# Loading a set of attention rows by one transfer, and paying with a stepped VectorE write

## The chip, the cores and the metric

The kernel runs on one core of one Trainium2 chip. The metric is device time in microseconds (us): the median of several executions of the whole program. Five engines work side by side, each taking its own instructions in a fixed order: TensorE (PE in the profile; its weight loads are PEld), VectorE (DVE), ScalarE (ACT), GpSimd (POOL) and SyncE (SP). They meet at semaphores. SP, ACT and POOL also issue transfers, which 16 shared DMA engines carry out.

## The reference

The program has two stages. The first is attention with hashed masking: `q`, `k`, `v` have 4 batches, 8 heads, 768 tokens, 64 features. Six projections of each `q` and `k` row give six sign bits, a query sees only the keys with the same six bits, and a softmax over these weights the values.

```
q_bits = (einsum('bhsd,dk->bhsk', q, proj) > 0)          # the same for k
mask   = q_bucket[:, :, :, None] == k_bucket[:, :, None, :]
scores = where(mask, (q @ k.T) / 8, -1e9)
attn   = softmax(scores);  x = attn @ v                   # heads side by side: 3072 x 512
h      = max(x @ w1, x @ w2, x @ w3)                      # 512 -> 768
out    = h @ w_out                                        # 768 -> 512
```

The second stage is a feed-forward block over the 3072 rows of `x`, with a maximum over three products in the place of an activation.

## The kernel before

**Sets.** The queries or the keys ("one side") of four heads make a set, and there are eight quads of heads, `g` = 0 to 7, two to a batch. Batch 0 (quads 0 and 1) is loaded and transposed in another way, by pairs of heads on TensorE. For quads 2 to 7 a set passes through these steps, and the change touches the first two:

- `load_quad` brings a set into a tile `nat` of 128 partitions, 32 for each head, with 24 tokens of 64 features in each partition. It does so with four transfers, one for each head (L194).
- `turn` (L200) is a VectorE stream transpose of 32x32 blocks, from `nat` to the tile T32, where features are on partitions and tokens run along the row. One turn writes 128x384 in fp32, so a set has four turns: two halves of the features by two halves of the tokens.
- `narrow` (L205) is a GpSimd pass that scales T32 to bf16, after every second turn.
- `place` (L210) sends the result by four transfers from SP into S, the operand of the score matmuls.
- `quad_hash` (L219) takes the turned tiles of both sides of a quad, computes their projections with eight matmuls on TensorE, has VectorE make bits of the signs (L222), and returns a function that sends the bits by four transfers from SP (L230) into eight extra rows of S. With those rows in the contraction, tokens of different buckets get scores that the exponential takes to almost nothing.

**Units.** The attention is cut into 192 units, 48 to a batch. A unit is one head with 768 columns of scores: two or three matmuls (L296) and one exponential on ScalarE (L304). Batch 0 has three chunks of 256 queries, the others two of 384. A loop over the units issues first the scores of the next unit, then whatever a table `at` holds for this unit, then pieces of the feed-forward block as a credit allows (L406 for the first layer, with VectorE's maxima at L415 and copies at L413; L450 for the second, with ScalarE's copies at L454), then sums (L351) and values (L373) of heads that are done, and last the hash, if `hash_at` names one for this unit. Sums of weights over tokens are prepared by VectorE (L327, L330), and VectorE also divides (L358 to L380).

The order of every engine is thus written out by hand: `when(u, ...)` puts a step at a unit, and the position in the loop is the position in each engine's queue. A load of quads 4 to 7 is issued by POOL, 14 to 11 units ahead of the set's first turn, one head to a unit; the loads of quads 2 and 3 come from SP, but for the queries of quad 2, which come from POOL. The turns of quads 4 to 7 are spread at two and a quarter or three units from each other (`SPREAD`). The hash of quad 3 stands at unit 48, behind the sums and values that end batch 0. Its bits are first needed by unit 60, whose scores are issued at unit 59.

**Buffers that matter.** Four PSUM banks (`bank`, `give`) serve all matmuls except the scores: TensorE can begin a group only when VectorE or ScalarE has emptied the bank that comes free next. The scores have two PSUM buffers of their own. `nat` has six buffers, T32 and its bf16 copy three each, S six.

Of the kernel before, what the change touches and what calls it, by code (L numbers as in the profile page):

```python
# [17 lines left out]
def kernel(  # L18
# [12 lines left out]
    nc = tc.nc  # L31
    B, H, S, D = q.shape
# [3 lines left out]
    HALF = S // 2  # L36
# [4 lines left out]
    Q = 32  # L41
    CC = P // Q
# [55 lines left out]
    nat, t32, t16, s_of, where, v_at = {}, {}, {}, {}, {}, {}  # L98

    def start_set(name, heads):  # L100
        nat[name] = nat_pool.tile([P, 4 * NM * D], FP32, tag="nat", name="nat")
        for x, key in enumerate(heads):
            where[key] = (name, x)
# [7 lines left out]
    def load_pair(pi, eng, sides=(1, 0), h0=0, h1=2):  # L111
        if pi not in nat:
            start_set(pi, [(0, 2 * pi), (0, 2 * pi + 1), (1, 2 * pi), (1, 2 * pi + 1)])
        n = nat[pi].rearrange("p (s h w) -> p s h w", s=2, h=2)
        for side in sides:
            src = (q, k)[side][0, 2 * pi + h0 : 2 * pi + h1].rearrange("h (p c) d -> p h (c d)", p=P)
            eng.dma_start(n[:, side, h0:h1, :], src)
# [66 lines left out]
        give(i)  # L184


    def load_quad(side, g, xs, eng):
        if (side, g) not in nat:
            start_set((side, g), [(side, 4 * g + x) for x in range(4)])
        for x in xs:  # L190
            b, h = divmod(4 * g + x, H)
            src = (q, k)[side][b, h].rearrange("(cc t m) d -> t cc (m d)", cc=CC, t=Q)
            dst = nat[side, g][x * Q : (x + 1) * Q, :].rearrange("t (cc w) -> t cc w", cc=CC)
            eng.dma_start(dst, src)  # L194

    def turn(name, u, half):
        if name not in t32:
            t32[name] = t32_pool.tile([P, 2, S], FP32, tag="T32", name="T32")
        i_ = nat[name].rearrange("p (cc m u d) -> p u m cc d", cc=CC, u=2, d=Q)[:, u, half * MH : (half + 1) * MH]
        nc.vector.transpose(t32[name][:, u, half * HALF : (half + 1) * HALF], i_)  # L200

    def narrow(name, u):
        if name not in t16:
# [268 lines left out]
    def when(u, f, *args):  # L472
        at.setdefault(u, []).append(lambda: f(*args))

    with tc.manual_schedule():
# [7 lines left out]
        load_pair(1, nc.sync)  # L483
        load_pair(2, nc.sync)
        load_pair(3, nc.sync)
        load_quad(1, 2, range(4), nc.sync)
        nc.vector.memset(pj2[:], 0.0)
        nc.vector.memset(ones[:], 1.0)
        for t in at_tiles:
# [67 lines left out]
        when(17, load_v, 1)  # L557
        for n, u in ((0, 3), (1, 12), (2, 21), (3, 31)):
            when(u, load_weights, n)
        when(13, load_quad, 0, 2, range(4), nc.gpsimd)  # L560
        for u, side, g in ((23, 1, 3), (27, 0, 3)):
            when(u, load_quad, side, g, range(4), nc.sync)
        hash_at = {}
        for g in range(2, NQUAD):
            b2, i2 = divmod(g, 2)
            need = UPB * b2 + 12 * i2
            for n, side in enumerate((1, 0)):
                name = (side, g)
                if g > 3:
                    us = [SPREAD[b2][0] + SPREAD[b2][1] * (8 * i2 + 4 * n + n2) // 4 for n2 in range(4)]  # L570
                    for x in range(4):
                        when(us[0] - 14 + x, load_quad, side, g, (x,), nc.gpsimd)
                else:
                    us = [need - {2: 26, 3: 23}[g] + 4 * n + n2 for n2 in range(4)]
                for n2, u2 in enumerate(us):
                    when(u2, turn, name, n2 // 2, n2 % 2)
                    if n2 % 2:
                        when(u2 + 1, narrow, name, n2 // 2)
                when(us[3] + 3, place, name, range(4))
            hash_at[{2: 32, 3: 48, 4: need - 12}.get(g, need - 9)] = g  # L580
            when({2: 36, 3: 46}.get(g, need - 22), load_v, g)

        ffn, credit = [], 0
# [2 lines left out]
        for c, i in sorted(done_at, key=lambda e: done_at[e]):  # L586
            d = done_at[c, i] + LAG[c > 2]
            sums, values = burst(c, i)
            pieces = [lambda f=sums: f(0, NM), lambda f=values: f(0, 0, NM), lambda f=values: f(1, 0, NM)]
            for n, f in enumerate(pieces):  # L590
                u = {(0, 0): (16, 17, 20), (1, 0): (21, 22, 24), (2, 0): (26, 27, 29)}.get((c, i), (d, d, d))[n]
# [67 lines left out]
```

## Time and profile before

| What | Value |
|---|---|
| median of 3 executions | 268.19 us (267.94 to 268.28) |
| the profiled execution, its own time | 268.58 us |
| span of its instructions | 266.6 us |
| busy PE / DVE / ACT / POOL | 257.9 / 208.9 / 177.3 / 69.9 us |
| the 48 turns (L200) on DVE | 27.0 us busy, 565 ns each |
| the 36 set loads issued by POOL (L194) | 20.0 us busy, 560 ns each |
| mean DMA rate over the span | 116 GB/s |
| granted TensorE clock | 1.0 |

Between the profiled execution's own time and its span lie 1.98 us, ahead of the first instruction and behind the last. The profiled execution is 0.39 us over the median. How to read the rest: a group line gives source line, engine, operation, shape and count, then total busy time and the mean time of one; waits name the engine that came last by the profile; the chain is what ended last, followed back in time from the last instruction. Busy times of a window table are sums within each stretch of the span.

### The profile page before, as it was taken

What the parts mean: (1) busy time and instruction counts of PE and PEld (TensorE: products, weight loads), DVE (VectorE), ACT (ScalarE), POOL (GpSimd) and SP (SyncE); (2) the same over time, 40 slices, a digit from 0 to 9 for tenths busy, and PEclk for the clock granted to TensorE, in tenths of its full rate; (3) what the DMA queues carried; (4) which work ended last, traced back from release to release, by engine and by line L of the source; (5) the groups of instructions that cost most, each with busy time, mean ns of one, the idle gap of its engine ahead of it and who ended that gap; (6) DMA issues with size and microseconds to landing.
All of it is one profiled execution on the core that took longest, in us unless ns stands there. A gap on an engine that the chain in (4) does not pass through costs nothing.

```text
span 266.6 us, 6482 instructions
## 1 busy us (share of the span) xinstructions
PE 257.9 (97%) x2505; PEld 154.4 (58%) x2505; DVE 208.9 (78%) x493; ACT 177.3 (67%) x257; POOL 69.9 (26%) x132
## 2 busy tenths in 40 slices
PE   7899999999799999999999999999999999999995
PEld 4555557885566575555555554555555555554552
DVE  2897685987499999978998997899849785888361
ACT  3596785676758694984869578484895859581322
POOL 3588652355032535240141612011000000000000
PEclk9999999999999999999999999999999999999999
DMA  6977999969703791982054472802030003000303
GB/s 203 316 156 135 230 234 212 245 114 233 185 22 86 159 231 18 234 222 53 4 167 131 56 182 43 204 8 61 15 118 4 0 2 119 2 0 2 118 0 118
DMA packets 20717, 30.95 MB, mean 116 GB/s; under 512 B 2608, under 2 KB 15248, under 8 KB 20688
## 3 DMA queue, kind: packets, MB, share of 16 engines
q0 software_dynamic: 8128, 13.37, 26.6%
q1 hardware_dynamic: 12128, 16.66, 21.8%
q10 hardware_dynamic: 432, 0.52, 0.6%
q8 instruction: 19, 0.31, 0.5%
q14 instruction: 10, 0.08, 0.1%
HBM read 25.17 MB, written 6.29 MB: 118 GB/s over the span
## 4 chain that ended last, share of the span: by engine, by line
PE 84%; DVE 7%; ACT 5%; issue 3%; DVEq 0%; ACTq 0%
PE ms L406 31%; PE sc L296 21%; PE ms L373 11%; PE ms L450 10%; ACT AT L304 4%; PE ms L351 3%; PE ms L219 3%; DVE ht L415 2%; DVE ad L327 1%; PE ms L498 1%; PE ms L122 1%; PE ms L149 1%; DVE T L131 1%; PE ms L169 1%; DVE S L174 1%
## 5 line engine op out<-in xcount | busy, mean ns | idle before, releaser
L304 ACT ACTIVATE AT<-sc 128x768 f16<-128x768 f32 x192 | 152.3, 816 | 62.2 <-PE sc L296 60.7
L406 PE MATMUL ms<-xT,w_sb 128*128 128x384 f16 (+1 forms) x648 | 114.8, 307 | 0.1
L296 PE MATMUL sc<-S 72*128 72x384 bf16 (+1 forms) x432 | 93.6, 308 | 3.3 <-ACT AT L304 1.8
L406 PEld LDWEIGHTS <-w_sb 128*128 128x128 f16 x648 | 62.7, 97 | 35.9 <-issue 0.4
L415 DVE TENSOR_TENSOR ht<-ht,ms 128x384 f16<-128x384 f16 (+1 forms) x108 | 54.3, 504 | 24.4 <-PE ms L406 13.4
L296 PEld LDWEIGHTS <-S 72*128 72x128 bf16 (+1 forms) x432 | 39.4, 98 | 35.7 <-issue 15.5
L205 POOL TENSOR_SCALAR T<-T 128x768 bf16<-128x768 f32 x24 | 22.8, 952 | 95.4 <-issue 50.5
L450 PE MATMUL ms<-wout_sb,ht 128*128 128x512 f16 x138 | 35.5, 378 | 0.0
L373 PE MATMUL ms<-AT,vo 128*32 128x385 f16 (+3 forms) x864 | 35.2, 309 | 0.3 <-DVE ht L415 0.3
L327 DVE TENSOR_TENSOR ad<-ad,AT 128x768 f16<-128x768 f16 x48 | 26.6, 553 | 2.1 <-ACT AT L304 1.3
L373 PEld LDWEIGHTS <-vo 128*32 128x32 f16 x864 | 22.6, 96 | 9.6 <-issue 1.8
L200 DVE STREAM_TRANSPOSE T<-nat 128x384 f32<-128x384 f32 x48 | 27.0, 565 | 0.2 <-DMA nat<-in_q_dram 0.2
L327 DVE TENSOR_TENSOR ad<-AT,AT 128x768 f16<-128x768 f16 x48 | 26.2, 546 | 0.2 <-ACT AT L304 0.2
L411 ACT CAST ht<-ms 128x384 f16<-128x384 f32 x36 | 17.3, 479 | 8.1 <-PE ms L406 8.1
L380 DVE SCALAR_TENSOR_TENSOR xT<-ms,sv,rb 128x384 f16<-128x384 f32 (+1 forms) x36 | 19.8, 567 | 1.4
L450 PEld LDWEIGHTS <-ht 128*128 128x128 f16 x138 | 13.3, 97 | 13.0 <-issue 0.3
L454 ACT COPY osb<-ms 128x512 f32<-128x512 f32 x21 | 12.2, 585 | 8.2 <-PE ms L450 6.3
L330 DVE TENSOR_TENSOR ad<-ad 128x384 f16<-128x384 f16 x32 | 15.5, 484 | 1.1
L136 POOL TENSOR_SCALAR S<-T 64x384 bf16<-64x384 f32 (+1 forms) x23 | 14.2, 617 | 5.0 <-DVE T L131 3.5
L358 DVE STREAM_TRANSPOSE ys<-ms 128x384 f32<-128x384 f32 (+1 forms) x18 | 9.6, 532 | 6.2 <-PE ms L351 6.2
L194 POOL DMA_DIRECT2D nat<-in_q_dram x20 | 11.1, 560 | 0.1
L413 DVE CAST ht<-ms 128x256 f16<-128x256 f32 x18 | 7.4, 413 | 4.0 <-PE ms L406 3.9
(48 smaller groups left out, 123.0 us busy)
## 6 DMA issues: line engine op xcount, KB each, us to landing
out_dram<-osb SPq DMA_DIRECT2D x21, 256.0 KB
S<-T SPq DMA_DIRECT2D x48, 96.0 KB
nat<-in_q_dram POOLq DMA_DIRECT2D x20, 192.0 KB, 6.7
vo<-in_v_dram POOLq DMA_DIRECT2D x8, 384.0 KB, 6.2
nat<-in_k_dram POOLq DMA_DIRECT2D x16, 192.0 KB, 5.7
w_sb<-in_moe_w_dram POOLq DMA_DIRECT2D x3, 768.0 KB, 6.9
nat<-in_k_dram SPq DMA_DIRECT2D x10, 192.0 KB
nat<-in_k_dram SPq DMA_DIRECT2D x3, 384.0 KB
```

The costliest lines, as they stand in the source:

```text
L200: nc.vector.transpose(t32[name][:, u, half * HALF : (half + 1) * HALF], i_)
L205: nc.gpsimd.tensor_scalar(out=t16[name][:, u, :], in0=t32[name][:, u, :], scalar1=RS, scalar2=1.0, op0=AluOp.mult, op1=AluOp.mult)
L296: nc.tensor.matmul(views[j], s_of[kn][0 : D + bits, kx, m * P : (m + 1) * P], s_of[qn][0 : D + bits, qx, q0 : q0 + w], start=True, stop=True)
L304: nc.scalar.activation(t[:, :, 0:w], whole, ActFn.Exp, bias=-SCALE * 0.25 * bits, scale=SCALE)
L327: nc.vector.tensor_tensor(out=sum_of[c, h][:], in0=t[0], in1=t[n], op=AluOp.add)
L330: nc.vector.tensor_tensor(out=t[:, 0, :], in0=t[:, 0, :], in1=t[:, 1, :], op=AluOp.add)
L373: nc.tensor.matmul(av[Q * x : Q * (x + 1), 0:n], v_at[2 * b + i][:, x, cb * D + side : (cb + 1) * D : 2], weights_of(c, 4 * i + x, m)[:, 0 ...
L380: nc.vector.scalar_tensor_tensor(out=xt_of(c)[:, 2 * i + side, 0:w], in0=av[:, 0:w], scalar=sv_of[b, i, side][:], in1=rb[0][:, 0:w], op0=A ...
L406: nc.tensor.matmul(ps[:, 0:w], w_sb[wi][:, jc, fb * P : (fb + 1) * P], xt[:, jc, 0:w], start=(jc == 0), stop=(jc == NJC - 1))
L411: nc.scalar.copy(hts[fb][:, 0:w], ps[:, 0:w])
L415: nc.vector.tensor_tensor(out=hts[fb][:, 0:w], in0=hts[fb][:, 0:w], in1=ps[:, 0:w], op=AluOp.max)
L450: nc.tensor.matmul(ps[:, 0:DM], hts[fb][:, tb * P : (tb + 1) * P], wout_sb[:, fb, :], start=(fb == 0), stop=(fb == NFB - 1))
```

## The change

A set is loaded by one transfer. A partition of `nat` now holds 24 tokens that follow one another in memory (6 KB in one piece), where before it held four groups of six tokens, 192 tokens apart (four pieces of 1.5 KB). The token that a partition and place hold is therefore another one; for S to keep its order, `turn` now writes its blocks interleaved: successive elements of a row go to addresses four fp32 words apart, in place of next to each other. Reads, shapes and everything behind T32 stay as they are.

The one transfer of quads 4 to 7 is issued 13 units ahead of the first turn, and the hash of quad 3 goes from unit 48 to unit 47, which puts its eight matmuls and its VectorE step ahead of the sums and values that end batch 0.

```diff
-    def load_quad(side, g, xs, eng):
-        if (side, g) not in nat:
-            start_set((side, g), [(side, 4 * g + x) for x in range(4)])
-        for x in xs:
-            b, h = divmod(4 * g + x, H)
-            src = (q, k)[side][b, h].rearrange("(cc t m) d -> t cc (m d)", cc=CC, t=Q)
-            dst = nat[side, g][x * Q : (x + 1) * Q, :].rearrange("t (cc w) -> t cc w", cc=CC)
-            eng.dma_start(dst, src)
+    def load_quad(side, g, eng):
+        start_set((side, g), [(side, 4 * g + x) for x in range(4)])
+        b, h = divmod(4 * g, H)
+        eng.dma_start(nat[side, g][:], (q, k)[side][b, h : h + 4].rearrange("h (t m) d -> (h t) (m d)", t=Q))
...
-        nc.vector.transpose(t32[name][:, u, half * HALF : (half + 1) * HALF], i_)
+        o = t32[name][:, u, half * HALF : (half + 1) * HALF].rearrange("p (m t cc) -> p m cc t", cc=CC, t=Q)
+        nc.vector.transpose(o, i_)
...
-        load_quad(1, 2, range(4), nc.sync)
+        load_quad(1, 2, nc.sync)
...
-        when(13, load_quad, 0, 2, range(4), nc.gpsimd)
+        when(13, load_quad, 0, 2, nc.gpsimd)
         for u, side, g in ((23, 1, 3), (27, 0, 3)):
-            when(u, load_quad, side, g, range(4), nc.sync)
+            when(u, load_quad, side, g, nc.sync)
...
-                    for x in range(4):
-                        when(us[0] - 14 + x, load_quad, side, g, (x,), nc.gpsimd)
+                    when(us[0] - 13, load_quad, side, g, nc.gpsimd)
...
-            hash_at[{2: 32, 3: 48, 4: need - 12}.get(g, need - 9)] = g
+            hash_at[{2: 32, 3: 47, 4: need - 12}.get(g, need - 9)] = g
```

On VectorE's queue the order of the steps is unchanged but for the one hash step (L222), which moves from behind the division of the last burst of batch 0 to ahead of it. POOL issues 9 set loads in place of 36, SP 3 in place of 12.

## The prediction

> **What bounds the kernel now.** I read the page's first parts, then who waits for whom, then the chain in order of time, then busy times by stretch.
>
> ```profile
> span 266.6 us, 6482 instructions
> ...
> PE 257.9 (97%) x2505; PEld 154.4 (58%) x2505; DVE 208.9 (78%) x493; ACT 177.3 (67%) x257; POOL 69.9 (26%) x132
> ...
> PE   7899999999799999999999999999999999999995
> PEld 4555557885566575555555554555555555554552
> DVE  2897685987499999978998997899849785888361
> ```
>
> PE is full but for the start, the end and one dent, slice 10 of the second part (about 67 to 73 us). A change can gain only there, or lose by holding PE up. The waits of PE between 60 and 80 us name the dent:
>
> ```profile
> PE sc L296 <- ACT AT L304: 1.5, 1, 1.5
> ```
>
> The chain shows the same place, and what comes behind it (start, duration, what):
>
> ```profile
> 70.13 0.82 ACT AT L304
> 70.95 1.00 issue
> 71.95 0.48 PE sc L296 x2
> 74.05 0.57 DVE T L200
> 76.44 0.49 DVE T L200
> 77.71 0.50 DVE ys L358
> ```
>
> ACT is named, but its last exponential ended at 70.95, and PE went on a whole microsecond later. The scores that start at 71.95 are those of unit 60, the first to need quad 3. SP issued that quad's four bit transfers (L230) only from 62.08 to 65.02 us, with the DMA engines saturated (share 1.09 between 60 and 70 us); the trace's semaphore records have the third of them, the first query bits, complete at 71.86. So the bits end the wait. Second, the turn itself (L200) stands on the chain right behind. Busy times by stretch of DVE say why; the columns are the stretch, its length, then PE, PEld, DVE, ACT and POOL with counts:
>
> ```profile
> 80.00:90.00 10.00, 9.85 (x68) 6.33 (x66) 9.76 (x23) 9.08 (x14) 3.67 (x5) 1.00 0.43 124
> 90.00:100.00 10.00, 10.00 (x119) 7.07 (x122) 9.72 (x26) 7.12 (x10) 3.98 (x6) 1.00 0.89 190
> 100.00:110.00 10.00, 10.00 (x116) 5.88 (x113) 9.48 (x24) 5.62 (x8) 4.03 (x6) 1.00 0.49 87
> ```
>
> DVE is as full as PE there. Its 58 us of idle time lie elsewhere.
>
> **The change part by part.**
>
> *The hash at unit 47.* Eight matmuls (1.29 us on the chain at 60.13) move ahead of a sums-and-values burst; TensorE does the same work. VectorE's bit step (554 ns) passes that burst's division; the division is late by that and by the 1.29 us, but its consumer, the feed-forward of that chunk, starts only at 67.6, seven microseconds on, which covers it. In front of the hash PE now stands at 58.03. The last turn that it needs ended at 55.73, so with turns as they are the bits would be made near 59.9, and SP, busy with the place transfers until 59.47, would issue them at about 60.0, not 62.08. That is 2.1 us earlier, the third transfer would land near 69.8, and the 1.48 us of PE waiting at 70.47 would vanish. Bounds: 0 to -1.48.
>
> *One transfer for four.* POOL loses 36 issues of 560 ns (20.0 us busy) and gains nine. One costs between 0.56 us (the issue of 128 rows, L194 now) and 0.81 us (512 rows, L238), 5 to 7 us in all. POOL's next work after most loads is the narrow pass, which idles 95 us in total before it starts, so I cost the saving at nothing. In the one crowded stretch, 25.7 to 29.7 us, two S writes (L136) start about 1.5 us earlier; nobody on PE waits for POOL there (the waits from 16 to 52 us have no such row). SP loses nine issues, median 0.31 to 0.43 us each; those at 31.8 to 36.9 lie before a place step that waits for POOL anyway (40.36), and the first four, from 6.4 us on, are ahead of bit transfers that SP issues only at 25.46. The loads are the same bytes. They start between one unit later and two units earlier; at quad 4's queries the load now stands behind eight memsets (L388, last at 60.7) and still goes about a microsecond before the time when its quarters went (62.17 to 64.35). A turn waits for a load once in the whole trace, 0.22 us. Cost 0, from -0.2 up to +1.5, the whole dent, if larger packets hold up the bits.
>
> *The stepped write.* 48 turns write fp32 words 16 bytes apart. No VectorE row of the trace does this at length.
>
> ```profile
> L200 DVE STREAM_TRANSPOSE T<-nat 128x384 f32<-128x384 f32 x48 | 27.0, 565 | 0.2 <-DMA nat<-in_q_dram 0.2
> ...
> L362 DVE STREAM_TRANSPOSE rb<-rr 128x384 f32<-128x384 f32 x12 | 6.9, 579 | 0.4
> ...
> L360 DVE TENSOR_SCALAR rr<-ys 128x12 f32<-128x12 f32 x12 | 2.1, 175 | 0.4
> ...
> L362 DVE STREAM_TRANSPOSE rb<-rr 128x256 f32<-128x256 f32 x6 | 2.7, 445 | 0.2
> ...
> L360 DVE TENSOR_SCALAR rr<-ys 128x8 f32<-128x8 f32 x6 | 1.0, 171 | 0.2
> ```
>
> A dense transpose costs (579 - 445)/128 = 1.05 ns an element. The low end is L360, which *reads* with a step of 32 words: four more elements cost 4 ns, 1.0 ns each, so a step would be free. The high end is GpSimd's copy into the projection tile (L536), the only row that *writes* fp32 with this step of four: 12 elements in 196 ns, against 182 ns for six with a step of two (L493), 2.3 ns an element, where GpSimd's dense pass takes (825 - 506)/384 = 0.83. That is 1.5 ns extra, 0.58 us for 384 elements. A gain is excluded: the dense write already runs at the pace of every other fp32 row. I take a row that writes as nearer than one that reads. But its 14 ns include the change of rows in a tiny copy, so I take a doubled pace, 1.05 ns extra: 0.40 us a turn, 19 us of VectorE time.
>
> [...]
>
> What of it reaches PE? I add the turns' extra to each stretch's DVE time and count what exceeds 10 us. The same stretches, turns alone:
>
> ```profile
> 80.00:90.00 10.00, 2.85 (x5) 1.00 0.43 124
> 90.00:100.00 10.00, 1.71 (x3) 1.00 0.89 190
> 100.00:110.00 10.00, 1.69 (x3) 1.00 0.49 87
> ```
>
> With 1.14 in 70 to 80 us, the turns hold 7.39 us from 70 to 110; at 0.40/0.565 of that, 5.23 us come on top. Idle DVE there: 0.34 (2.23 less the 1.89 that it waits through the dent) + 0.24 + 0.28 + 0.52 = 1.38. Excess 3.85 us. From 110 to 190 us the stretches' idle times are 1.52, 0.91, 0.63, 0.83, 0.48, 2.07, 0.50 and 1.05, the turns' extras 1.20, 0.92, 1.09, 1.22, 0.81, 0.80, 1.21 and 0.40; the excess is 0.01 + 0.46 + 0.39 + 0.33 + 0.71 = 1.90. PE waits for VectorE's bank, with everything queued behind, scores included; it has no idle time later to take this back. Before 70 us: 30 to 40 us has eight turns, 8.03 + 3.02, over by 1.05; the next stretch, 7.26 busy, takes it up, and PE itself leaves 0.60 and 0.21 there. Cost 0, at worst 1.05.
>
> The stepped turns also eat part of the hash's gain: four end 1.6 us later, so narrow, place and bits go 1.6 later on SP's queue than 56.65, 59.47 and 60.0 suggest. Bits start at about 60.9, 1.2 us earlier than before. I take -1.2.
>
> **Sum**, against the profiled execution's own 268.58: -1.2 + 3.85 + 1.90 = 273.13. That execution lies 0.39 over the median of the three, so the forecast is 272.7 us.
>
> **Rivals.**
>
> 1. *The stepped write is free* (the L360 reading). Then only the dent goes: 268.58 - 1.48 - 0.39 = 266.7 us, faster. It decides below 0.21 us extra a turn: there the turns from 70 to 110 us add 2.7, less 1.38 idle, and the later stretches 0.1, which is about the dent's 1.48. For it: stepped reads run at full pace. Against: the only row that writes with the step is slow. [...] Chance 0.23.
> 2. *VectorE's idle time hides the slower turns.* DVE is idle 57.7 us, three times the 19 us. Time 268.58 - 1.2 - 0.39 = 267.0. Against: the order is fixed, and where the turns stand the idle time is 2 to 5 in 100. It would need PE to run ahead by several groups, which four banks forbid. Chance 0.04.
> 3. *A dear step.* At 0.58 us, the same count gives 6.2 + 4.5, the bits move by only 0.5, and 268.58 + 10.7 - 0.5 - 0.39 = 278.4. Chance 0.23.
> 4. *A mild step,* 0.25 us: 1.89 + 0.33 and the full 1.48 back: 269.4 - 0.4 = 269.0. Chance 0.2.
> 5. *The bits still land late* because 6 KB packets take their turns among them: forecast plus 1.2, 273.9; it goes with any of the others, and I give it 0.3 inside them.
>
> The forecast itself, 0.40 give or take 0.08, holds 0.3. Below 266.6 nothing leads; the dear end is cut at 277.5, so 266.6 to 277.5 leaves out somewhat under 2 in 10. Given a price for the step, the range is 268.7 to 278. This kernel's three executions differ by 0.13%, so 0.2% is about what can be told from no change. Faster 0.25 (rivals 1 and 2, less their edge), same 0.04 (a step near 0.2 us), slower 0.71.
>
> **What would show it.** The turns' mean duration in the group table decides most: 565 ns now, near 965 forecast, under 770 rival 1. PE should wait on VectorE (L415, L413 or L380 as releaser) between 74 and 110 us, with DVE at 10 of 10 there. The dent at 71 us should shrink to about 0.3 us, and L219's second group should start near 58 us. POOL's set loads should be nine. If the turns are slow and PE stays full, the step that failed is the count of excess by stretch; if the turns are fast and the time rises anyway, it is the transfers.

## The result and the profile after

The changed kernel takes 272.57 us (272.23 to 272.83, four executions) against 268.24 us (267.94 to 268.51, four): 1.0156 times as long, with a 95% interval of 1.0137 to 1.0175. The forecast was 272.7 us. The sum met the time, but, as the runs below show, not all of its terms did. The profiled execution takes 272.73 us, its span 271.0.

The page's first parts, of the changed kernel:

```profile
span 271.0 us, 6430 instructions
...
PE 261.0 (96%) x2505; PEld 155.1 (57%) x2505; DVE 219.3 (81%) x493; ACT 177.5 (66%) x257; POOL 54.2 (20%) x105
...
PE   8899999999998989999999999998999999999995
...
DVE  2797696987799999998999999799848885788361
```

The dent of PE in slice 10 is gone, and new ones stand at slices 12 and 14 (81 to 88 and 95 to 101 us). Busy times by stretch (columns as before: PE, PEld, DVE, ACT, POOL) put numbers to it:

```profile
70.00:80.00 10.00, 10.00 (x117) 7.09 (x116) 9.37 (x24) 7.14 (x10) 1.50 (x2) 1.00 0.21 60
80.00:90.00 10.00, 9.08 (x61) 5.64 (x60) 9.79 (x21) 8.15 (x13) 2.32 (x3) 1.00 0.34 110
90.00:100.00 10.00, 9.40 (x110) 6.35 (x109) 9.82 (x24) 6.30 (x9) 1.91 (x3) 1.00 0.80 198
100.00:110.00 10.00, 9.76 (x116) 5.84 (x115) 9.59 (x23) 5.00 (x7) 3.27 (x4) 1.00 0.30 45
```

From 80 to 110 us VectorE was at 9.48 to 9.76 of 10 before and had next to nothing left; now PE is the one that has idle time. PE's waits between 70 and 110 us name one releaser, VectorE's maxima of the feed-forward block, which free the PSUM banks:

```profile
PE ms L403 <- DVE ht L412: 1.4, 3, 0.6
```

In the kernel before there was no such row. The row names 1.4 us, and PE idles 1.76 in all in these 40 us; the loss read from the table below, 2.94, is larger, and the profile does not show where the rest of it lies. The group rows give the turn's price:

```profile
L197 DVE STREAM_TRANSPOSE T<-nat 128x384 f32<-128x384 f32 x48 | 40.9, 862 | 0.0
```

It is 862 ns, where it was 565: 0.30 us more, between the mild case (0.25) and the forecast (0.40).

To see where each kernel loses, I take from the traces the start of the exponential of the same unit in each kernel, less that of the kernel before, in us. The first row has the starts of the kernel before themselves. The differences at unit 0 come and go from run to run and mean nothing. Each row is one execution: `e2_before_hash47` and `e5_quads23`, whose medians agree within 0.04 us, end 1.8 us apart here, and single steps of two kernels can differ by half a microsecond. Only steps that several kernels share are to be relied on.

```
unit                  0     48     58     64     96    112    120    140    160    191
before             8.61  56.93  69.37  76.03 114.13 134.94 145.98 173.55 198.60 239.22
changed            0.29   0.39   0.85  -0.78   2.16   2.16   2.86   3.02   4.29   4.29
e1_hash48          0.07   0.18   0.18  -1.28   1.64   1.64   2.41   2.57   3.83   3.83
e2_before_hash47  -0.37  -0.40  -0.16  -1.79  -1.79  -1.79  -2.07  -2.07  -2.07  -2.07
e3_dense_one_load -0.13   0.11   0.35  -1.29  -1.29  -1.29  -0.80  -0.81  -0.50  -0.50
e4_step_four_loads 0.30   0.29   0.73  -0.91   2.02   2.02   2.22   2.78   3.68   3.68
e5_quads23         0.16   0.66   1.11  -0.53  -0.53  -0.53  -0.28  -0.28  -0.28  -0.28
e6_quads45        -0.27  -0.28  -0.03  -1.67   1.27   1.27   1.44   1.44   1.75   1.75
e7_quads67         0.21   0.19   0.43  -1.20  -1.20  -1.20  -0.81  -0.53   0.41   0.41
e10_filler30       0.07   1.09   1.68   0.05   3.16   3.16   3.37   3.96   4.92   4.92
e11_dense_hash48   0.07   0.10   0.10  -1.54  -1.55  -1.55  -0.53  -0.53  -0.23  -0.23
e12_four_loads_67 -0.14   0.40   0.40  -1.24  -1.24  -1.24  -1.07  -1.07  -1.00  -0.99
```

The changed kernel's row reads: 0.46 us lost between units 48 and 58, 1.63 won at unit 60 (the dent), 2.94 lost by unit 96, 0.70 by unit 116 (0.47 of it at unit 113, a step that the kernels with stepped turns and four transfers have too), and 1.43 more, most of it at unit 149.

### The profile page after: what moved, and what is told of

Same layout as the page of the kernel before. It is cut to its first block, busy times and chain, and to the rows that moved or that the text cites. A ratio compares the mean times of both kernels' runs of the same rounds, so it can differ in the third digit from the quotient of the medians.

```text
span 271.0 us, 6430 instructions
## 1 busy us (share of the span) xinstructions
PE 261.0 (96%) x2505; PEld 155.1 (57%) x2505; DVE 219.3 (81%) x493; ACT 177.5 (66%) x257; POOL 54.2 (20%) x105
## 4 chain that ended last, share of the span: by engine, by line
PE 69%; DVE 19%; issue 5%; ACT 3%; DMA 2%; DVEq 0%; ACTq 0%
PE ms L403 25%; PE sc L293 17%; PE ms L370 9%; PE ms L447 9%; DVE T L197 5%; DVE ht L412 4%; DVE ad L324 4%; PE ms L216 2%; ACT AT L301 2%; PE ms L348 2%; DMA out_dram<-osb 2%; PE ms L122 1%; PE ms L495 1%; DVE xT L377 1%; DVE ht L410 1%
## 5 line engine op out<-in xcount | busy, mean ns | idle before, releaser
L202 POOL TENSOR_SCALAR T<-T 128x768 bf16<-128x768 f32 x24 | 22.0, 916 | 116.2 <-DVE T L197 72.6
L197 DVE STREAM_TRANSPOSE T<-nat 128x384 f32<-128x384 f32 x48 | 40.9, 862 | 0.0
L324 DVE TENSOR_TENSOR ad<-ad,AT 128x768 f16<-128x768 f16 x48 | 27.2, 566 | 2.1 <-ACT AT L301 1.3
L174 DVE TENSOR_SCALAR S<-ms 6x384 bf16<-6x384 f32 x16 | 8.9, 554 | 2.3 <-PE ms L169 2.0
```

The source lines that it names most:

```text
L197: nc.vector.transpose(o, i_)
L202: nc.gpsimd.tensor_scalar(out=t16[name][:, u, :], in0=t32[name][:, u, :], scalar1=RS, scalar2=1.0, op0=AluOp.mult, op1=AluOp.mult)
L324: nc.vector.tensor_tensor(out=sum_of[c, h][:], in0=t[0], in1=t[n], op=AluOp.add)
```

## The experiments

My theory (A in the expectations) was that the stepped write is the loss, through VectorE's time alone, and the hash's earlier place the gain, with the transfers worth nothing. Rivals gave the transfers a part (B, C) or the stepped write an effect on others (E).

**Undoing one part: the hash back at 48**

```diff
-            hash_at[{2: 32, 3: 47, 4: need - 12}.get(g, need - 9)] = g
+            hash_at[{2: 32, 3: 48, 4: need - 12}.get(g, need - 9)] = g
```

> The changed kernel with the hash of quad 3 put back to unit 48. Theory A (the hash move alone removed the wait at 71 us, the transfers gave nothing): the wait of PE before unit 60's scores is back with 1 to 1.5 us, and the time is 1.2 to 1.6 us over the changed kernel's 272.6: about 274.0. Theory B (the single transfers let the bits land earlier, so the hash's place does not matter): the time stays at 272.6, give or take 0.4, and PE does not wait there.

Measured: 272.43 us (272.26 to 272.56), and in the trace no wait of PE at all from 60 to 80 us. Theory A falls here. The dent is gone with the hash where it always was (-1.46 from unit 58 to 64), and the time is the changed kernel's, as theory B has it.

**One part alone: the hash at 47 in the kernel before**

```diff
-            hash_at[{2: 32, 3: 48, 4: need - 12}.get(g, need - 9)] = g
+            hash_at[{2: 32, 3: 47, 4: need - 12}.get(g, need - 9)] = g
```

> The kernel before with nothing but the hash of quad 3 at unit 47. Theory A: PE's wait of 1.5 us before unit 60 goes, and the time falls from 268.2 to about 266.8. Theory B: the bits still land late among the small transfers, the wait stays over 0.7 us, and the time is 267.6 or more.

Measured: 267.31 us (266.50 to 268.09, ten executions), 0.995 of the kernel before, interval 0.9927 to 0.9973. Here theory A holds on the wait, which is gone; the time is 0.5 us over its 266.8, but under theory B's 267.6. With four transfers a set, the hash's place alone removes the dent (-1.63): SP issues the bits from 58.95 us instead of 62.08. No kernel with the right result was faster in this study by more than the runs scatter.

**The transfers alone, with and without the hash's move.** Two kernels load a set by one transfer but write the turn densely, so that the tokens stand in another order in S than in the values: all the work is there, the attention is of wrong pairs.

```diff
-        o = t32[name][:, u, half * HALF : (half + 1) * HALF].rearrange("p (m t cc) -> p m cc t", cc=CC, t=Q)
-        nc.vector.transpose(o, i_)
+        nc.vector.transpose(t32[name][:, u, half * HALF : (half + 1) * HALF], i_)
...
-            hash_at[{2: 32, 3: 47, 4: need - 12}.get(g, need - 9)] = g      (second kernel only)
+            hash_at[{2: 32, 3: 48, 4: need - 12}.get(g, need - 9)] = g
```

> The changed kernel with turns that write next to each other again, and the set still loaded by one transfer; tokens then stand in another order in S than the values have, so this computes a wrong attention, with all the work of the kernel. Theory A (the stepped write is the whole loss): turns back at 565 ns, no PE wait on VectorE from 80 to 110 us, time 266.8, equal to the kernel before with the hash moved within 0.4. Theory C (the single transfer costs something by itself, by late loads or by holding up small transfers): over 267.5.

> One transfer a set, dense turns (wrong token order in S, all the work there), and the hash of quad 3 at unit 48 as before. Theory B (the single transfers by themselves let the bits land in time): no wait of PE over 0.4 us before unit 60, time as with the hash at 47 and one transfer, 268.1 within 0.5. Theory A (only the hash's place counts; the changed kernel with the hash at 48 escaped because its slow turns shifted the loads): PE waits 1 us or more before unit 60, time about 269.4.

Measured: 268.13 us (267.33 to 270.95) with the hash at 47, 268.09 (267.02 to 268.45) with it at 48. The second has the dent gone too (-1.64), so theory B is right for these kernels: the single transfers by themselves let the bits land in time. SP issues the bits at 62.18 us, no earlier than in the kernel before (62.08), but by the semaphore records the third of their transfers is complete at 69.06 us, not at 71.86. The reason is in the stretches around the bits; the last two columns are the busy share of the DMA engines and what they moved, in GB/s. The kernel before, then the one with single transfers, dense turns and the hash at 48:

```profile
62.00:66.00 4.00, 4.00 (x28) 2.49 (x27) 3.19 (x8) 3.83 (x5) 2.35 (x5) 1.00 1.07 217
66.00:70.00 4.00, 4.00 (x29) 2.56 (x28) 1.46 (x4) 3.83 (x7) 0.00 (x0) 1.00 1.02 216
```

```profile
62.00:66.00 4.00, 4.00 (x28) 2.52 (x26) 3.28 (x8) 3.79 (x5) 0.00 (x0) 1.00 1.04 351
66.00:70.00 4.00, 4.00 (x29) 2.55 (x27) 1.37 (x5) 3.83 (x7) 0.00 (x0) 1.00 0.61 208
```

At about the same share of busy DMA engines, rows of 6 KB go through at 351 GB/s where rows of 1.5 KB went at 217, and the queue empties sooner (share 0.61 against 1.02). The packets themselves say the same: from 62 to 66 us a load's packets of 4,608 bytes take 342 ns each in the kernel before, those of 6,144 bytes 282 ns in the other (286 in the changed kernel). Whether the longer rows do this or the smaller number of transfers, the runs do not separate.

But the first of the two kernels is 0.8 us slower than the hash's move alone (268.13 against 267.31), on theory C's side of 267.5, and both lose near unit 115, 0.5 and 1.0 us. So the single transfers seem to cost something as well. The difference is small: as ratios to the kernel before the two are 1.0006 (0.9978 to 1.0035) and 0.9971 (0.9951 to 0.9990), where the hash's move alone has 0.995 (0.9927 to 0.9973).

**Where that cost comes from.** PE's wait there, in the kernel with the hash at 48 (130 to 150 us), is on ScalarE, and ScalarE stands behind its own output copy, ahead of which it sits idle for 1.6 us. The profile names PE for that; in the kernel with the hash at 47 the same copy waits 1.1 us for an output transfer. PE's row, hash at 48:

```profile
PE sc L292 <- ACT AT L300: 1.1, 1, 1.1
```

The last run leaves single transfers for quads 2 to 5 and gives quads 6 and 7 four again; the single load of quad 6's keys, which is issued at about 134 us, is then gone. The turns are dense and the order wrong for quads 2 to 5.

```diff
+    ONE = (2, 3, 4, 5)
...
+            if g in ONE:
+                b, h = divmod(4 * g, H)
+                eng.dma_start(nat[side, g][:], (q, k)[side][b, h : h + 4].rearrange("h (t m) d -> (h t) (m d)", t=Q))
-        for x in xs:
+        for x in xs if g not in ONE else ():
...
+                    if g in ONE:
+                        when(us[0] - 13, load_quad, side, g, (), nc.gpsimd)
-                    for x in range(4):
+                    for x in range(4) if g not in ONE else ():
```

> Dense turns, hash of quad 3 at unit 48, one transfer a set for quads 2 to 5 (tokens in wrong order there), four for quads 6 and 7 as before. With one transfer everywhere PE lost 1.0 us at units 113 to 116, near 142 us, where ScalarE waits for an output transfer beside the load of quad 6's keys. Theory H (the single load of quad 6 delays that output transfer): no loss there, 267.0 to 267.2, a microsecond under the one with single transfers everywhere (268.1). Theory I (it is a coincidence of timing, which the kernels with four transfers show too): a loss of 0.3 us or more stays, time 267.5 or more.

Measured: 266.94 us (266.36 to 268.48), 0.9919 of the kernel before (0.9886 to 0.9952), and PE's wait there shrinks:

```profile
PE sc L301 <- ACT AT L309: 0.3, 1, 0.3
```

The loss near unit 115 falls from 1.02 to 0.17 us. By its time this is theory H's side: what the single transfers cost seems to go with those of quads 6 and 7. The waits don't bear out how. The kernels below that have single transfers for quads 2 and 3 alone, or 4 and 5 alone, give quad 6 four transfers and still have this wait of PE, 0.4 and 0.3 us, each behind a wait of ScalarE of 0.8 us for an output transfer. The one with single transfers for quads 6 and 7 alone has the single load and no wait of PE here. So the load of quad 6's keys does not decide it, and why the two kernels above lose 0.5 and 1.0 us is open.

**The stepped write alone**

```diff
-        nc.vector.transpose(t32[name][:, u, half * HALF : (half + 1) * HALF], i_)
+        o = t32[name][:, u, half * HALF : (half + 1) * HALF].rearrange("p (m t cc) -> p m cc t", cc=CC, t=Q)
+        nc.vector.transpose(o, i_)
...
-            hash_at[{2: 32, 3: 48, 4: need - 12}.get(g, need - 9)] = g
+            hash_at[{2: 32, 3: 47, 4: need - 12}.get(g, need - 9)] = g
```

> The kernel before with the hash at unit 47 and the stepped write, but four transfers a set with tokens laid as before, so the tokens' order in S is wrong and the attention with it; all the work is there. Theory A: turns at 860 ns, time 272.6 as the changed kernel, within 0.5. Theory C: the time differs from the changed kernel's by more than 0.5, by what the transfers are worth.

Measured: 272.11 us (271.97 to 272.71), turns at 862 ns. Over the kernel with the hash moved alone that is 4.8 us, and it is nearly all of the changed kernel's loss. Theory A's margin of 0.5 just holds (272.6 against 272.11).

**Which turns cost.** Three kernels have single transfers and stepped turns for two quads only, the hash at 47, and give the right result:

```diff
+    ONE = (2, 3)          # then (4, 5), then (6, 7); load_quad and its calls as above
...
+        if name[1] in ONE:
+            o = t32[name][:, u, half * HALF : (half + 1) * HALF].rearrange("p (m t cc) -> p m cc t", cc=CC, t=Q)
+            nc.vector.transpose(o, i_)
+            return
         nc.vector.transpose(t32[name][:, u, half * HALF : (half + 1) * HALF], i_)
```

> The single transfer and the stepped turns for quads 2 and 3 alone (16 turns, all before 60 us), the others as in the kernel before, hash of quad 3 at unit 47. Theory A (the slower turn costs only where VectorE is full, from 74 us on): the same as the kernel before with the hash moved, 267.3, within 0.5. Theory D (the early turns cost too, since they delay the sets): 268.0 or more, with PE behind by 0.5 us or more at unit 60.

> The same for quads 4 and 5 alone (16 turns, some 74 to 128 us). The changed kernel lost 2.9 us of position against the kernel before between units 64 and 96. Theory A: these turns alone give that loss, 267.3 + 2.9 = 270.2, all of it between units 64 and 100. Theory F (VectorE's lateness adds up over the kernel, so half the turns cost much less than half): under 269.0.

> The same for quads 6 and 7 alone (16 turns, some 128 to 186 us). The changed kernel lost 2.1 us between units 96 and 152. Theory A: 267.3 + 2.1 = 269.4, with the largest single step, over 1 us, at units 144 to 150, where the last turns stand just ahead of quad 7's hash. Theory F: under 268.5.

Measured: 267.35 us (266.79 to 268.45), 270.14 (269.81 to 270.93) and 268.78 (268.30 to 269.86). Against 267.31, sixteen turns, with the single transfers of their sets, cost nothing, 2.8 us and 1.5 us according to where they stand. Theory A is right on the first two within 0.1; the third is 0.6 under its number but over theory F's. The three together make 4.3 of the 5.26 us between the changed kernel and the one with the hash moved alone. Quad 7's part comes in one step of 0.94 us at unit 149, where the last turns stand just ahead of that quad's hash.

**VectorE's time without the step.** Plain writes behind every dense turn, to tiles that nobody uses any more:

```diff
         nc.vector.transpose(t32[name][:, u, half * HALF : (half + 1) * HALF], i_)
+        nc.vector.memset(iden[:], 0.0)
+        nc.vector.memset(iden[:], 0.0)
+        nc.vector.memset(pj2[:], 0.0)
```

> The kernel before with the hash at unit 47, dense turns, and behind every turn three plain writes by VectorE to tiles that are no longer used (128x128 twice, 128x32), about 0.28 us together. Theory A (the loss is VectorE's time and nothing else): 267.3 + 4.6, about 272, with PE losing at the same units as the changed kernel. Theory E (the stepped write disturbs others, by its accesses to memory): under 270.

Measured: 281.56 us (281.12 to 281.84). It overshot because the filler did: of two writes to the same tile the second starts 0.25 us after the first (VectorE idles 4.5 us in all ahead of the 48 second writes), where with two tiles it is 0.14 us and no idle time stands there, and from a turn's start to the next step it is 0.93 us in the place of 0.49, 0.44 more and not 0.28. The second filler writes to two tiles:

```diff
+    fill = konst.tile([P, P], FP32, name="fill")
...
         nc.vector.transpose(t32[name][:, u, half * HALF : (half + 1) * HALF], i_)
+        nc.vector.memset(iden[:], 0.0)
+        nc.vector.memset(fill[:], 0.0)
```

> The filler again, now two plain writes to two tiles behind every dense turn (128x128 each), about 0.30 us together where the first filler took 0.44; hash at 47, four transfers. Theory A (VectorE's time alone): as the stepped turns with four transfers, 272.1, within 0.7. Theory E (the stepped write also disturbs others): under 271.0.

Measured: 272.94 us (272.46 to 273.86), 1.0140 of the kernel before (1.0103 to 1.0177) where the stepped turns with four transfers have 1.0143 (1.0116 to 1.0171). It misses the margin in microseconds by 0.1 and agrees as a ratio. In the second filler's trace, VectorE from one turn to what follows:

```profile
76.67 0.57 DVE L201 STREAM_TRANSPOSE T<-nat 128x384 f32<-128x384 f32 x1
77.22 0.17 DVE L202 MEMSET iden<- 128x128 f32 x1
77.36 0.17 DVE L203 MEMSET fill<- 128x128 f32 x1
77.44 0.49 DVE L330 TENSOR_TENSOR ad<-AT,AT 128x768 f16<-128x768 f16 x1
```

That is 0.77 us. In the changed kernel the same distance is 0.71 us (median of 13 turns from 70 to 112 us; 0.49 before): the turn lasts 0.30 longer, but takes only 0.22 more of the queue, since the next step starts before the turn's end (at 76.57 us, behind a turn from 75.82 to 76.73). PE waits in both at the same instructions (the maxima of the feed-forward block, 1.6 and 1.4 us). So VectorE's time alone makes a loss of this size; an effect on others is not needed, and theory E's number (under 271.0) falls. A small effect is not excluded, since the filler takes 0.28 us of the queue and the stepped write 0.22.

**The price by itself.** One run, executed once, has only the operations, eight of each, and gives zeros as output:

```
for _ in range(REPS):                                    # step 1, 2, 3, 4, 6, 12
    nc.vector.transpose(dst[:].rearrange("p (m t cc) -> p m cc t", cc=4, t=32), src[:])
...
nc.vector.transpose(dst[:].rearrange("p (t cc w) -> p cc t w", t=16, w=2), src[:])     # pairs
```

> Not the program but its parts: eight VectorE transposes of 128x384 fp32 each with a write step of 1, 2, 3, 4, 6 and 12 words and one that writes pairs 24 words apart, then plain VectorE copies that write with a step of 1, 4, 12 or read with a step of 4, 12, then GpSimd copies that write with a step of 1 and 4; the output is zeros. Theory A (every word that does not follow its neighbour costs about 0.8 ns): 565 ns dense, 860 at every step over 1, pairs at 565. Theory G (the cost grows with the distance): 565 dense, under 700 at step 2, 860 at 4, over 1000 at 12. Reads with a step, from the row that read ys: no extra.

Its group rows, in order of lines: L37 dense, L39 to L47 steps of 2, 3, 4, 6 and 12, L49 pairs 24 words apart; then VectorE copies: L51 dense, L53 and L55 writing with steps of 4 and 12, L57 and L59 reading with them; then GpSimd copies, L61 dense, L63 writing with a step of 4.

```profile
L63 POOL COPY dst<-dst 128x384 f32<-128x384 f32 x8 | 6.9, 859 | 0.5
L45 DVE STREAM_TRANSPOSE dst<-src 128x384 f32<-128x384 f32 x8 | 6.8, 854 | 0.3
L43 DVE STREAM_TRANSPOSE dst<-src 128x384 f32<-128x384 f32 x8 | 6.8, 853 | 0.3
L47 DVE STREAM_TRANSPOSE dst<-src 128x384 f32<-128x384 f32 x8 | 6.8, 845 | 0.3
L53 DVE COPY dst<-src 128x384 f32<-128x384 f32 x8 | 6.6, 828 | 0.3
L57 DVE COPY dst<-src 128x384 f32<-128x384 f32 x8 | 6.6, 828 | 0.3
L41 DVE STREAM_TRANSPOSE dst<-src 128x384 f32<-128x384 f32 x8 | 5.5, 686 | 0.3
L49 DVE STREAM_TRANSPOSE dst<-src 128x384 f32<-128x384 f32 x8 | 5.2, 646 | 0.3
L37 DVE STREAM_TRANSPOSE dst<-src 128x384 f32<-128x384 f32 x8 | 4.6, 579 | 1.7 <-DMA src<-in_q_dram 1.4
L39 DVE STREAM_TRANSPOSE dst<-src 128x384 f32<-128x384 f32 x8 | 4.6, 579 | 0.3
L61 POOL COPY dst<-dst 128x384 f32<-128x384 f32 x8 | 4.1, 506 | 70.4 <-DVE dst L59 69.9
L55 DVE COPY dst<-src 128x384 f32<-128x384 f32 x8 | 4.0, 501 | 0.3
L59 DVE COPY dst<-src 128x384 f32<-128x384 f32 x8 | 4.0, 496 | 0.3
L51 DVE COPY dst<-src 128x384 f32<-128x384 f32 x8 | 2.9, 360 | 0.3
```

Both theories miss. A transpose pays nothing at a step of two (579), a third of the price at three (686), all of it at four (853), and no more at six and twelve (854 and 845). The pairs, 24 words apart, pay 67 ns (646), and a plain copy pays less at a step of twelve (501 writing, 496 reading) than at four (828 both). What makes these prices, the runs do not show.

## Why the prediction was right, and where it was not

*What bounds the kernel* stands. VectorE was full where the slower turns cost most (9.48 to 9.76 of 10 us busy from 80 to 110 us), PE had no reserve (9.85 to 10.00 there), and the idle time that VectorE has elsewhere did not help. The rival that idle time hides the turns is refuted by the quads: sixteen turns cost 0, 2.8 or 1.5 us, by the place where they stand.

*The turn's price* was oversized: 0.40 us forecast, 0.30 measured (0.22 of the queue). The bounds of 0 and 0.58 held it. The row that read with a step (four more elements, 4 ns) misled as the low end: its step is 32 words, which no run measured at length, and at length a read with a step of four costs a plain copy as much as such a write (828 ns both). GpSimd's tiny copy was too high as the other end: at length GpSimd pays (859 - 506)/384 = 0.92 ns an element, not 1.5. The doubled pace, 1.05 ns extra an element, was my choice between these ends, and no row of the kernel before shows it; at length a transpose pays (853 - 579)/384 = 0.71. The mild case's 0.25 us a turn was a price set between free and doubled, which no row shows either; the measured 0.30 lies nearer to it than to the forecast.

*The count of excess by stretch* was undersized, and this made good for the price. With 0.30 a turn it gives 2.5 us from 70 to 110 and 0.8 after, 3.3; the positions lose 2.94 and then 0.70 + 1.43. So the total was luck in part: at the measured price the prediction's own count would have made 268.58 - 1.2 + 3.3 - 0.39 = 270.3 us. The failing step is the 1.38 us of idle time from 70 to 110 us that I let the turns fill first. Between the exponentials of units 64 and 96 VectorE runs the same 87 instructions in both kernels, in 38.10 us before and 41.04 in the changed one, and idles 1.32 and 1.39 us of that, in gaps of at most 0.105 us: none of the idle time was used. It is the small change between instructions. The fifteen turns there take 15 x 0.22 = 3.3 us more of the queue, and 2.94 are lost; the count is good to some tenths only (the second filler takes about 4 us more there and loses 3.11). After unit 96 idle time did help: up to unit 150 it shrinks from 7.19 to 4.98 us, and 2.13 us are lost. But a step of about 1 us at unit 149, on a hash right behind its last turn, no sum over ten microseconds could see.

*The hash at unit 47* was right about what the dent is, and wrong in this kernel about who removes it. Moving the hash removes it where sets come by four transfers (267.31 us). The single transfers remove it as well, and with them the hash's move is worth nothing: 272.57 with it, 272.43 without. The gain of 1.2 was in the sum once and arrived once (1.63 in position, so it was undersized too); it just had two owners.

*One transfer for four, cost 0,* failed. The transfers are worth the dent, through 351 GB/s where there were 217. With dense turns the two kernels that have them everywhere also lose 0.5 and 1.0 us near 142 us, for a reason that stays open; in the changed kernel 0.23 us go there, as in kernels with four transfers for quad 6 (0.17 to 0.25). The rival that large packets hold up the bits is the wrong way round.

*The early turns, cost 0 and at worst 1.05*: the kernel with only those stepped takes 267.35, where the hash's move alone has 267.31. Between units 48 and 58 the changed kernel loses 0.46 us, where the earlier hash stands closely behind slower turns. With the hash at 47 and dense turns it is 0.24, with the hash at 48 nothing, so the hash's move has a small price that the sum left out.

## What to carry to other kernels

Price a slower instruction by the stretch in which it stands, and count as idle there only gaps in which a whole instruction waits for another engine; the gaps of a tenth of a microsecond between instructions hid nothing here. Before a layout change is paid with a step on VectorE, look whether a smaller step will do: a step of two fp32 words was free (579 ns, as dense), one of four cost a transpose half as much again (853). When a change holds two remedies for one wait, try each alone: here one of them, a single number, gives 267.3 us without the part that cost 4.8.

## What the runs showed that I had not expected

- Transposes of 128x384 fp32: 579 ns at write steps of one and two words, 686 at three, 853 at four, no dearer at twelve (845).
- Plain VectorE copies go from 360 ns dense to 828 at a step of four, whether it is the write or the read, and back to about 500 at a step of twelve (501 for the write, 496 for the read). Why twelve is cheaper than four for a copy and not for a transpose stays open.
- With loads of 128 rows of 6 KB among the other transfers the DMA engines moved 351 GB/s at the busy share (1.04) at which, with rows of 1.5 KB, they moved 217 (1.07).
- A turn that lasts 0.30 us longer took 0.22 us more of VectorE's queue; and the loss is not proportional: a filler of 0.28 us a turn cost 5.6 us over the hash's move alone, one of 0.44 us 14.3.
